# Block sums in 32-column tiles, row sums placed behind a GEMM 1 step, and the last output group in two column halves

## The chip, the core and the metric

The kernel runs on one core of a Trainium2 chip. The time is the device time of one execution in microseconds (us), the median over several executions. Beside it stands one execution that the hardware profiler recorded; all durations below are of that execution. The engines are called PE (matmuls), DVE (vector), ACT (scalar activation), POOL (GpSimd) and SP (Sync, which here only issues transfers).

## What is computed

Attention with a local part and a summary part feeds a two-layer network. There are 4 batches, 8 heads, 768 positions and 64 columns a head.

```python
k_sum = k.reshape(B, H, nb, block, D).max(axis=3)      # block = 32, nb = 24
v_sum = v.reshape(B, H, nb, block, D).mean(axis=3)
scores_l = scale * np.matmul(q, k.transpose(0, 1, 3, 2))
mask_l = np.abs(pos[:, None] - pos[None, :]) < window  # window = 16
scores_s = scale * np.einsum('bhsd,bhnd->bhsn', q, k_sum) + np.log(block)
a = softmax(np.concatenate([np.where(mask_l, scores_l, -1e9), scores_s], axis=-1))
attn = np.matmul(a, np.concatenate([v, v_sum], axis=2))
x = attn.transpose(0, 2, 1, 3).reshape(B * S, H * D)   # 3072 tokens x 512
h = x @ w_in                                           # 512 x 2048: GEMM 1
g = h * np.clip(h + 3.0, 0.0, 6.0) / 6.0
out = g @ w_out                                        # 2048 x 512: GEMM 2
```

A block's mean of v times 32 is its sum, so the kernel works with block sums of v and counts a block's weight 32 times in the denominator.

## The kernel before

**Tiles.** The 3072 tokens are 8 tiles of 384, two (the `half`s) for each batch b. Heads go in pairs p = 0 to 3, and pairs in groups g = 0 and 1. For a batch, `K` transposes k on PE, copies it into block-diagonal form (`kbd`) and takes block maxima (`red`, then `kst`); `Tq` transposes q; `Sl` makes local scores, the exponential on ACT and the mask on DVE; `Ss` makes the summary scores. `AV(b, p, half)` accumulates the numerator `num` and the denominator `den` in PSUM, takes 1/den on ACT as the exponential of a negated logarithm (lines 398 and 399) and writes x on DVE (line 400). `F1(t, ft)` is one of the 16 steps of GEMM 1 of tile t: four matmuls into `hp` (line 412), a Relu on ACT (line 415) and the product `g` on DVE (line 416). `F2` is GEMM 2: for each of three groups of 128 tokens, 16 accumulating matmuls of 512 columns (line 425), a copy on ACT (line 429) and a store that SP issues (line 431).

**Block sums of v.** They are needed as `vst[p]`, on 96 partitions (4 heads x 24 blocks) with the other heads' columns masked out, which `to_vst` does in two DVE operations (line 233). There are two ways to them.
- Batch 0: v is loaded in f32 by SP (`load_vf`, line 129) and summed on PE. `vsum0(p)` multiplies with an indicator `ind`; the two pairs of a group accumulate into an 8-partition result, in two PSUM tiles of 6 blocks' columns each. After the second pair, ACT and DVE copy one PSUM tile each into `vs8`, and SP issues one transfer that spreads it over 96 partitions, `vs96[g]` (line 266).
- Later batches: `load_vrows` brings rows of v in f32 (`vr`, 768 KB each, issued by POOL, line 136) and `vsum(b, g)` adds them up on DVE in six operations (lines 238 to 243), then calls `to_vst`. `vr` has two buffers, and `vs8` uses the same ones.

**Order of the work.** POOL's order is that of the program all the time, so a transfer that POOL issues stands behind everything that POOL is told earlier, waits included. Until line 479 the order of PE, ACT and DVE is also that of the program. After it, a planner orders these three engines. `plan` hangs pieces of attention at slots: slot 16n + i is the i-th step of the n-th entry of `work_list`, which is F1(0); F1(1) with F2(0); F2(1); F1(2); then F1(t) with F2(t-1) for t = 3 to 7; F2(7). The planner may draw a piece's instructions ahead of its slot. On every engine instructions then run in the order so fixed.

**Holding back transfers.** `hold_loads(src)` is a tiny POOL copy from `src`: POOL waits until `src` is there, and so do the transfers behind it. Before the change, line 434 waits for the last f32 piece of v; then come two pieces of w_in, the rest of q of batch 0, two pieces of w_in and four of w_out.

**PSUM.** `ps_h` (2 buffers: `hp`), `ps_o` (2 buffers: GEMM 2 results, and some `num`/`den` of batch 0), `ps_s` (2), `ps_n` (one `num`, one `den`). In batch 0, `alt` in `AV` selects `ps_o` in place of `ps_n`.

Of the kernel before, what the change touches and what calls it, by code (L numbers as in the profile page):

```python
# [16 lines left out]
D = 64  # L17
# [15 lines left out]
def kernel(  # L33
# [173 lines left out]

    ind = const.tile([128, 2, 2, 4], F32, tag="ind", name="ind")
    nc.vector.memset(ind[:], 0.0)
    for i in range(4):  # L210
        for par in range(2):
            nc.vector.memset(ind[32 * i:32 * i + 32, par, par, i:i + 1], 1.0)
    for p in range(NP):
# [31 lines left out]


    def vcast(p):
        for j in range(2):
            rows = slice(64 * j, 64 * j + 64)
            (nc.vector.tensor_copy if j else nc.scalar.copy)(vbd[p][rows, :, rows], vf[p][rows])  # L250

    vps, vs96 = {}, {}

    def vsum0(p):
        g, par = p // 2, p % 2
        for h in range(2):
            if par == 0:
                vps[g, h] = ps_n.tile([8, NK // 2, D], F32, tag=("num", "den")[h], name="vps")
            nc.tensor.matmul(vps[g, h][:], ind[:, par].rearrange("p a b -> p (a b)"),  # L259
                             vf[p][:, h * (NK // 2):(h + 1) * (NK // 2)], start=(par == 0), stop=(par == 1))  # L260
        if par == 1:
            a = ld.tile([8, NK, D], F32, tag="vr", name="vs8", bufs=2)
            for h in range(2):
                (nc.vector.tensor_copy if h else nc.scalar.copy)(a[:, h * (NK // 2):(h + 1) * (NK // 2)], vps[g, h][:])
            vs96[g] = work.tile([RS, D], F32, tag="vs96", name="vs96")
            nc.sync.dma_start(out=vs96[g][:], in_=a[:])

# [103 lines left out]
    def AV(b, p, half):  # L371
# [3 lines left out]
        a, asm = at[p], asum[b, p // 2, half]  # L375
        alt = b == 0 and (half == 0 and p != 2 or half == 1 and p % 2 == 1)
        pool = ps_o if alt else ps_n
# [24 lines left out]

    gt, ops = {}, {}

    def F1(t, ft, wide):

        if ft == 0:
            gt[t] = gp.tile([128, NFT, HALF], BF16, tag="g", name="g")
        pool, tag = (ps_o, "o") if wide and ft % 2 else (ps_h, "h")
        hp = pool.tile([128, HALF], F32, tag=tag, name="hp")  # L410
        for kt in range(NP):
            nc.tensor.matmul(hp[:], w_in_sb[:, kt, ft * 128:(ft + 1) * 128], xt[t][:, kt],  # L412
                             start=(kt == 0), stop=(kt == NP - 1))
        r = hw.tile([128, HALF], F32, tag="r", name="r")
        nc.scalar.activation(r[:], hp[:], AF.Relu, bias=half_c[:], scale=1.0 / 6.0)  # L415
        nc.vector.scalar_tensor_tensor(gt[t][:, ft], r[:], 1.0, hp[:], op0=ALU.min, op1=ALU.mult)  # L416

    def F2(t, i, by_ft=False):

        ft, ts = (i // 3, i % 3) if by_ft else (i % NFT, i // NFT)  # L420
        if ft == 0:
            pool, tag = (ps_h, "h") if by_ft and ts == 2 else (ps_o, "o")
            ops[t, ts] = pool.tile([128, d_model], F32, tag=tag, name="op")
        op = ops[t, ts]
        nc.tensor.matmul(op[:], gt[t][:, ft, ts * 128:(ts + 1) * 128], w_out_sb[:, ft],  # L425
                         start=(ft == 0), stop=(ft == NFT - 1))
        if ft == NFT - 1:
            o = hw.tile([128, d_model], F32, tag="ot", name="ot")
            nc.scalar.copy(o[:], op[:])  # L429
            row = t * HALF + ts * 128  # L430
            nc.sync.dma_start(out=out[row:row + 128], in_=o[:])


    hold_loads(vf[NP - 1][:, 0, 0:1])
    load_w_in(0)
    load_w_in(1)
    load_q(0, 0, 4, 1)
    for c in range(2, 4):
        load_w_in(c)
    for c in range(4):  # L440
        load_w_out(c)

# [4 lines left out]
    def v_first(p):  # L447
        vsum0(p)
        vcast(p)

    zero_rest()
# [9 lines left out]
    S_first(1)  # L461
    nc.vector.tensor_scalar_mul(osum4[:], hm4[:], float(BLK))
    to_vst(0, vs96[0][:])
    K(0, 2)
    v_first(2)
    Tq(0, 2, 0)
    Ss(0, 0, 0)
    v_first(3)
    K(0, 3)
    Tq(0, 3, 0)  # L470
    S_first(2)
    AV(0, 0, 0)
    S_first(3)
    to_vst(1, vs96[1][:])
    AV(0, 1, 0)
    Ss(0, 1, 0)
    AV(0, 2, 0)
# [15 lines left out]

    def attention(b, t_slot, t_gap, av_slot, av_gap, loads):
        for p in range(NP):
# [10 lines left out]
            if p % 2 == 1:  # L506
                at_slot(s + 2, lambda g=p // 2: Ss(b, g, 0))
                at_slot(s + 3, lambda g=p // 2: Ss(b, g, 1))
                at_slot(s, lambda g=p // 2: vsum(b, g))
                if b + 1 < B:  # L510
                    at_slot(s, lambda g=p // 2: load_vrows(b + 1, g))
            if 2 <= b + 1 < B:
                at_slot(s + 1, lambda p=p: (load_k(b + 1, p), load_q(b + 1, p)))
        for i, (p, half) in enumerate(((0, 0), (1, 0), (2, 0), (3, 0), (0, 1), (1, 1), (2, 1), (3, 1))):
            at_slot(av_slot(i), lambda p=p, half=half: AV(b, p, half))
# [5 lines left out]
    for g in range(2):  # L521
        at_slot(11.5, lambda g=g: (load_k(1, 2 * g, 2), load_q(1, 2 * g, 2)))
        at_slot(15, lambda g=g: load_v(1, g))
        at_slot(15, lambda g=g: load_vrows(1, g))
    attention(1, 28, 3, lambda i: (41, 42, 45, 46, 50, 52, 54, 56)[i], 2, None)
    for b in range(2, B):
        base = 48 + 32 * (b - 2)
        order = (14, 16, 24, 26, 18, 20, 28, 30)
        attention(b, base, 5, lambda i, base=base: base + order[i], 2, None)

# [42 lines left out]
```

## Time and profile before

| What | Value |
|---|---|
| Time, median of 6 runs (range) | 262.48 us (261.0 to 265.01) |
| The profiled execution: time, span | 262.66 us, 260.8 us |
| PE, ACT, DVE, POOL busy | 238.7, 167.9, 156.4, 65.3 us |
| Mean granted PE clock | 0.987 |
| GEMM 1 matmuls, 512 of 384 columns | four in 0.65 us where PE is full |
| GEMM 2 matmuls, 384 of 512 columns | three in 0.65 us where PE is full |
| First GEMM 1 matmuls of tile 0, last of tile 0 | 27.7 us, 50.5 us |
| GEMM 1 of tiles 1, 2, 3 | 50.6 to 80.0, 99.5 to 119.3, 120.1 to 149.0 us |
| GEMM 2 of tile 1 | 71.2 to 98.8 us |
| Last GEMM 2 matmul starts | 256.4 us |

The span runs from the first to the last instruction of the trace; the execution's time is measured around it and is 1.9 us longer. In the views, a row of instructions gives engine, line, operation, what it writes and reads, and in brackets how long the engine had been idle before it and what ended that. Matmul durations in the trace overlap, so the distance between starts says what PE really passes. A wait of an engine costs time only where something that sets the end stands behind it.

### The profile page before, as it was taken

The page shows a single profiled execution, that of the slowest core. Times are in us where ns is not written, and L with a number is a line of the kernel's source. Part 1 is how long each engine was busy: PE and PEld are TensorE (multiplying, and loading weights), DVE is VectorE, ACT ScalarE, POOL GpSimd, SP SyncE. Part 2 cuts the span into 40 slices and gives each one's busy share as a digit, 9 for nine tenths or more (in the row PEclk, how much of TensorE's full clock was granted, in tenths as well). Part 3 has the DMA queues.
Part 4 walks back from the last instruction along what each step waited for, and adds up shares of the span by engine and source line. Part 5 has one row for each costly group of instructions (what it writes and reads, how often), then busy time and mean ns, then how long its engine had stood idle before and what let it go on. Part 6 is the DMA issues. An engine that isn't in the chain of part 4 may idle for free.

```text
span 260.8 us, 5002 instructions
## 1 busy us (share of the span) xinstructions
PE 238.7 (92%) x1936; PEld 135.7 (52%) x1936; DVE 156.4 (60%) x362; ACT 167.9 (64%) x325; POOL 65.3 (25%) x97
## 2 busy tenths in 40 slices
PE   1775699999899979999799999999999999999993
PEld 1233456644455646666455555666655555555541
DVE  4779446633899576997994477658544444444400
ACT  8577369833687858998577557766856655555410
POOL 7219000755381501796820400000000000000000
PEclk9999679999999999999999999999999999999999
DMA  7989998599999941999991451101011111101122
GB/s 127 192 126 159 203 200 137 72 195 205 219 259 81 205 59 44 79 156 169 182 124 40 33 70 41 43 1 43 0 40 43 40 40 43 40 0 41 43 80 80
DMA packets 62711, 25.80 MB, mean 99 GB/s; under 512 B 51296, under 2 KB 58464, under 8 KB 62688
## 3 DMA queue, kind: packets, MB, share of 16 engines
q0 software_dynamic: 52752, 17.57, 60.8%
q1 hardware_dynamic: 9936, 7.92, 10.3%
q8 instruction: 15, 0.25, 0.4%
q14 instruction: 8, 0.07, 0.1%
HBM read 31.98 MB, written 6.29 MB: 147 GB/s over the span
## 4 chain that ended last, share of the span: by engine, by line
PE 66%; DMA 13%; DVE 11%; ACT 5%; issue 2%; POOL 2%; DVEq 0%; ACTq 0%; POOLq 0%
PE hp L412 26%; PE op L425 24%; DMA vr<-in_v_dram 7%; DMA vs<-vs 4%; DVE g L416 3%; PE num L382 3%; DMA qb<-in_q_dram 2%; PE num L380 2%; PE den L386 2%; PE den L389 2%; ACT r L415 2%; PE sl L344 2%; PE vps L259 1%; PE ss L354 1%; POOL vbd L120 1%
## 5 line engine op out<-in xcount | busy, mean ns | idle before, releaser
L412 PE MATMUL hp<-x,win 128*128 128x384 bf16 x512 | 105.3, 329 | 2.4 <-DVE g L416 2.0
L415 ACT ACTIVATE r<-hp,half_c 128x384 f32<-128x384 f32 x128 | 73.5, 580 | 46.4 <-PE hp L412 45.6
L425 PE MATMUL op<-wout,g 128*128 128x512 bf16 x384 | 101.0, 379 | 0.0
L416 DVE SCALAR_TENSOR_TENSOR g<-r,hp 128x384 bf16<-128x384 f32 x128 | 69.7, 551 | 46.9 <-ACT r L415 46.8
L412 PEld LDWEIGHTS <-win 128*128 128x128 bf16 x512 | 47.8, 98 | 37.1 <-issue 6.3
L425 PEld LDWEIGHTS <-g 128*128 128x128 bf16 x384 | 36.6, 98 | 32.5 <-issue 0.6
L400 DVE TENSOR_TENSOR x<-num,lg 128x384 bf16<-128x384 f32 x32 | 17.7, 554 | 23.5 <-ACT lg L399 22.2
L398 ACT ACTIVATE lg<-den 128x384 f32<-128x384 f32 x32 | 15.7, 491 | 18.4 <-PE den L393 9.9
L120 POOL DMA_DIRECT2D vbd<-in_v_dram x24 | 18.2, 779 | 36.0 <-PE num L382 32.8
L347 ACT ACTIVATE at<-sl 128x376 bf16<-128x376 f32 (+2 forms) x48 | 22.3, 487 | 5.6 <-PE sl L344 5.6
L429 ACT COPY ot<-op 128x512 f32<-128x512 f32 x24 | 13.8, 584 | 8.9 <-PE op L425 8.8
L348 DVE TENSOR_TENSOR at<-at,mask 128x376 bf16<-128x376 bf16 (+2 forms) x48 | 16.1, 348 | 3.8 <-ACT at L347 3.7
L344 PE MATMUL sl<-qT,kbd 128*128 128x94 bf16 x192 | 14.4, 207 | 3.2 <-DVE kbd L305 3.1
L399 ACT ACTIVATE lg<-lg 128x384 f32<-128x384 f32 x32 | 16.8, 525 | 0.9
L344 PEld LDWEIGHTS <-kbd 128*128 128x128 bf16 x192 | 11.7, 98 | 10.4 <-DVE kbd L305 3.4
L382 PEld LDWEIGHTS <-vbd 128*128 128x128 bf16 x224 | 13.2, 101 | 6.6 <-issue 3.2
L113 POOL DMA_DIRECT2D qb<-in_q_dram x16 | 13.4, 855 | 6.3 <-DMA vr<-in_v_dram 6.3
L382 PE MATMUL num<-at,vbd 128*128 128x94 bf16 (+2 forms) x224 | 14.4, 204 | 0.0
L113 POOL DMA_DIRECT2D kb<-in_k_dram x16 | 13.4, 852 | 0.2
L380 PE MATMUL num<-asum,vst 96*128 96x384 bf16 x32 | 10.8, 338 | 2.8 <-DVE x L400 1.6
L386 PE MATMUL den<-asum,osum 96*128 96x384 bf16 x32 | 10.7, 334 | 1.4 <-DVE x L400 1.4
L389 PE MATMUL den<-at,obd 128*128 128x384 bf16 x32 | 11.1, 345 | 0.0
(82 smaller groups left out, 206.8 us busy)
## 6 DMA issues: line engine op xcount, KB each, us to landing
out_dram<-ot SPq DMA_DIRECT2D x24, 256.0 KB, 2.0
vr<-in_v_dram POOLq DMA_DIRECT2D x6, 768.0 KB, 8.0
vbd<-in_v_dram POOLq DMA_DIRECT2D x24, 96.0 KB, 3.3
win<-in_moe_w_in_dram POOLq DMA_DIRECT2D x4, 512.0 KB, 8.9
wout<-in_moe_w_out_dram POOLq DMA_DIRECT2D x4, 512.0 KB, 17.4
vf<-in_v_dram SPq DMA_DIRECT2D x8, 192.0 KB, 8.9
kb<-in_k_dram POOLq DMA_DIRECT2D x16, 96.0 KB, 6.8
qb<-in_q_dram POOLq DMA_DIRECT2D x16, 96.0 KB, 6.4
```

Of the source, the lines that this page charges most:

```text
L113: nc.gpsimd.dma_start(out=t[:, :, j], in_=src[b, 2 * p + j].rearrange("(s p) d -> p s d", p=128))
L120: nc.gpsimd.dma_start(out=vall[rows, p, lo:hi, rows], in_=v[b, 2 * p + j].rearrange("(n k) d -> k n d", k=KB)[:, lo:hi])
L344: nc.tensor.matmul(sp[:, i * WIN:(i + 1) * WIN], kbd[p][:, t], qT[p][:, PAD - HALO + t * KB:PAD - HALO + t * KB + WIN], start=True, stop=True)
L347: nc.scalar.activation(a, sp[:, 0:n * WIN].rearrange("p (n c) -> p n c", c=WIN), AF.Exp, scale=scl)
L382: nc.tensor.matmul(num[:, lo:hi], vbd[p][:, t], a[:, t, off:off + hi - lo], start=False, stop=(i == len(bl) - 1))
L389: nc.tensor.matmul(d3, ones, a[:, t0:t1, HALO:HALO + KB], start=False, stop=False)
L399: nc.scalar.activation(lg[:], lg[:], AF.Exp, scale=-1.0)
L400: nc.vector.tensor_tensor(xt[s][:, p], num[:], lg[:], op=ALU.mult)
L412: nc.tensor.matmul(hp[:], w_in_sb[:, kt, ft * 128:(ft + 1) * 128], xt[t][:, kt], start=(kt == 0), stop=(kt == NP - 1))
L415: nc.scalar.activation(r[:], hp[:], AF.Relu, bias=half_c[:], scale=1.0 / 6.0)
L416: nc.vector.scalar_tensor_tensor(gt[t][:, ft], r[:], 1.0, hp[:], op0=ALU.min, op1=ALU.mult)
L425: nc.tensor.matmul(op[:], gt[t][:, ft, ts * 128:(ts + 1) * 128], w_out_sb[:, ft], start=(ft == 0), stop=(ft == NFT - 1))
```

## The change

- `ind` becomes 128 x 32, with one column in eight used. For each pair and each half of a head's 64 columns, `vsum0` makes one matmul into its own 32 partitions of one PSUM tile per group (tag `num` for group 0, `den` for group 1); nothing accumulates over pairs. One ACT copy of 128 x 384 takes the result, and two transfers of 32 columns each bring every eighth partition to `vs96[g]`. POOL issues them, except the first of group 1, which SP issues.
- The weight loads and the rest of q wait for both halves of `vs96[1]` in place of the last f32 piece of v.
- In the hand-ordered start, `to_vst(0)` moves behind K(0, 2), both `v_first(2)` and `v_first(3)` behind Ss(0, 0, 0), AV(0, 0, 0) and AV(0, 1, 0) forward, and `to_vst(1)` behind Ss(0, 1, 0). `alt` is true where p % 2 equals half, so consecutive pairs use different PSUM pools.
- `vsum` has slots of its own and may no longer be drawn ahead of the DVE operation of the GEMM 1 step that was told last (`issue_after`). Batch 1: 36 and 39 for 35 and 41; batch 2: 52.5 and 56.5 for 57 and 67; batch 3: 68.5 and 78.5 for 89 and 99. Both `load_vrows` of a batch stand at one slot: 12 for 15 (batch 1), 45 for 35 and 41 (batch 2), 60 for 57 and 67 (batch 3).
- The last token group of GEMM 2 is 32 matmuls of 256 columns, one column half after the other, each with its own PSUM tile, copy and store. The last half is copied by ACT and DVE together.

```diff
-    ind = const.tile([128, 2, 2, 4], F32, tag="ind", name="ind")
+    ind = const.tile([128, 32], F32, tag="ind", name="ind")
     nc.vector.memset(ind[:], 0.0)
     for i in range(4):
-        for par in range(2):
-            nc.vector.memset(ind[32 * i:32 * i + 32, par, par, i:i + 1], 1.0)
+        nc.vector.memset(ind[32 * i:32 * i + 32, 8 * i:8 * i + 1], 1.0)
...
     def vsum0(p):
         g, par = p // 2, p % 2
+        if par == 0:
+            vps[g] = ps_n.tile([128, NK, D // 2], F32, tag=("num", "den")[g], name="vps")
         for h in range(2):
-            if par == 0:
-                vps[g, h] = ps_n.tile([8, NK // 2, D], F32, tag=("num", "den")[h], name="vps")
-            nc.tensor.matmul(vps[g, h][:], ind[:, par].rearrange("p a b -> p (a b)"),
-                             vf[p][:, h * (NK // 2):(h + 1) * (NK // 2)], start=(par == 0), stop=(par == 1))
+            c = 2 * h + par
+            nc.tensor.matmul(vps[g][32 * c:32 * c + 32], ind[:], vf[p][:, :, h * (D // 2):(h + 1) * (D // 2)],
+                             start=True, stop=True)
         if par == 1:
-            a = ld.tile([8, NK, D], F32, tag="vr", name="vs8", bufs=2)
+            a = ld.tile([128, NK, D // 2], F32, tag="vr", name="vs8", bufs=2)
+            nc.scalar.copy(a[:], vps[g][:])
+            vs96[g] = work.tile([RS, D], F32, tag="vs96", name="vs96")
             for h in range(2):
-                (nc.vector.tensor_copy if h else nc.scalar.copy)(a[:, h * (NK // 2):(h + 1) * (NK // 2)], vps[g, h][:])
-            vs96[g] = work.tile([RS, D], F32, tag="vs96", name="vs96")
-            nc.sync.dma_start(out=vs96[g][:], in_=a[:])
+                (nc.sync if g == 1 and h == 0 else nc.gpsimd).dma_start(
+                    out=vs96[g][:, h * (D // 2):(h + 1) * (D // 2)], in_=a[64 * h:64 * h + 64:8])
...
-        alt = b == 0 and (half == 0 and p != 2 or half == 1 and p % 2 == 1)
+        alt = b == 0 and p % 2 == half
...
-        nc.vector.scalar_tensor_tensor(gt[t][:, ft], r[:], 1.0, hp[:], op0=ALU.min, op1=ALU.mult)
+        last_g[0] = nc.vector.scalar_tensor_tensor(gt[t][:, ft], r[:], 1.0, hp[:], op0=ALU.min, op1=ALU.mult)
...
+        if t == NTILE - 1 and ts == HALF // 128 - 1:
+            F2_last(op, row, ft)
+            return
...
-    hold_loads(vf[NP - 1][:, 0, 0:1])
-    load_w_in(0)
-    load_w_in(1)
-    load_q(0, 0, 4, 1)
-    for c in range(2, 4):
-        load_w_in(c)
-    for c in range(4):
-        load_w_out(c)
+    def F2_last(op, row, step):
+
+        t, w, ts_last = NTILE - 1, d_model // 2, "last"
+        for n in (2 * step, 2 * step + 1):
+            h, ft = n // NFT, n % NFT
+            cols = slice(h * w, (h + 1) * w)
+            if n == NFT:
+                ops[t, ts_last] = ps_h.tile([128, w], F32, tag="h", name="op")
+            p = op[:, 0:w] if h == 0 else ops[t, ts_last][:]
+            nc.tensor.matmul(p, gt[t][:, ft, HALF - 128:], w_out_sb[:, ft, cols],
+                             start=(ft == 0), stop=(ft == NFT - 1))
+            if ft == NFT - 1:
+                o = hw.tile([128, d_model], F32, tag="ot", name="ot")
+                if h == 0:
+                    nc.scalar.copy(o[:, 0:w], p)
+                else:
+                    nc.scalar.copy(o[:, 0:w // 2], p[:, 0:w // 2])
+                    nc.vector.tensor_copy(o[:, w // 2:w], p[:, w // 2:])
+                nc.sync.dma_start(out=out[row:row + 128, cols], in_=o[:, 0:w])
...
     def v_first(p):
         vsum0(p)
         vcast(p)
+        if p == NP - 1:
+            hold_loads(vs96[1][:, 0:1])
+            hold_loads(vs96[1][:, D // 2:D // 2 + 1])
+            load_weights()
...
+    K(0, 2)
     to_vst(0, vs96[0][:])
-    K(0, 2)
-    v_first(2)
     Tq(0, 2, 0)
     Ss(0, 0, 0)
+    v_first(2)
     v_first(3)
+    AV(0, 0, 0)
     K(0, 3)
     Tq(0, 3, 0)
     S_first(2)
-    AV(0, 0, 0)
+    AV(0, 1, 0)
     S_first(3)
+    Ss(0, 1, 0)
     to_vst(1, vs96[1][:])
-    AV(0, 1, 0)
-    Ss(0, 1, 0)
     AV(0, 2, 0)
     AV(0, 3, 0)
...
+    def vsum_in_turn(b, g):
+        with tc.issue_after(last_g[0].ins):
+            vsum(b, g)
...
-                at_slot(s, lambda g=p // 2: vsum(b, g))
-                if b + 1 < B:
-                    at_slot(s, lambda g=p // 2: load_vrows(b + 1, g))
...
+        for g in range(2):
+            at_slot(sums[g], lambda g=g: vsum_in_turn(b, g))
+            if b + 1 < B:
+                at_slot(rows, lambda g=g: load_vrows(b + 1, g))
...
-        at_slot(15, lambda g=g: load_vrows(1, g))
-    attention(1, 28, 3, lambda i: (41, 42, 45, 46, 50, 52, 54, 56)[i], 2, None)
+        at_slot(12, lambda g=g: load_vrows(1, g))
+    attention(1, 28, 3, lambda i: (41, 42, 45, 46, 50, 52, 54, 56)[i], (36, 39), 45)
...
-        attention(b, base, 5, lambda i, base=base: base + order[i], 2, None)
+        attention(b, base, 5, lambda i, base=base: base + order[i], (base + 4.5, base + 8.5) if b == 2 else (base - 11.5, base - 1.5), base + 12)
```

`load_weights()` issues the same loads in the same order as the removed lines.

More of the change, by code (lines that the diff above doesn't have):

```diff
@@ L403 @@
     gt, ops = {}, {}
+    last_g = [None]
     def F1(t, ft, wide):
@@ L424, in F2 @@
         op = ops[t, ts]
+        row = t * HALF + ts * 128
+        if t == NTILE - 1 and ts == HALF // 128 - 1:
+            F2_last(op, row, ft)
+            return
         nc.tensor.matmul(op[:], gt[t][:, ft, ts * 128:(ts + 1) * 128], w_out_sb[:, ft],
@@ L429, in F2, with load_weights @@
             nc.scalar.copy(o[:], op[:])
-            row = t * HALF + ts * 128
             nc.sync.dma_start(out=out[row:row + 128], in_=o[:])
-    hold_loads(vf[NP - 1][:, 0, 0:1])
-    load_w_in(0)
-    load_w_in(1)
-    load_q(0, 0, 4, 1)
-    for c in range(2, 4):
-        load_w_in(c)
-    for c in range(4):
-        load_w_out(c)
+    def F2_last(op, row, step):
[16 more added lines that the diff above has]
+                nc.sync.dma_start(out=out[row:row + 128, cols], in_=o[:, 0:w])
+    def load_weights():
+        for c in range(2):
+            load_w_in(c)
+        load_q(0, 0, 4, 1)
+        for c in range(2, 4):
+            load_w_in(c)
+        for c in range(4):
+            load_w_out(c)
     def S_first(p):
@@ L492, with attention @@
         at_slot(12 + p, lambda p=p: AV(0, p, 1))
-    def attention(b, t_slot, t_gap, av_slot, av_gap, loads):
+    def vsum_in_turn(b, g):
+        with tc.issue_after(last_g[0].ins):
+            vsum(b, g)
+    def attention(b, t_slot, t_gap, av_slot, sums, rows):
         for p in range(NP):
```

## Prediction, made before the changed kernel ran

> **What bounds the kernel now.** I read four views, in this order: the busy table by stages, the chain that ended last, the list of waits, and the timeline around the waits. The busy table by stage says which engine is short where (columns: stage in us and its length; busy us and, in brackets, instructions of PE, weight loads, DVE, ACT, POOL; granted clock; DMA share; GB/s).
>
> ```profile
> 20.00:32.40 12.40, 7.53 (x99) 5.26 (x99) 8.31 (x20) 6.85 (x14) 5.47 (x8) 0.85 1.15 187
> 32.40:50.00 17.60, 17.42 (x186) 10.66 (x185) 10.81 (x22) 14.26 (x30) 2.58 (x5) 0.91 0.82 131
> 68.00:85.00 17.00, 16.77 (x163) 9.08 (x163) 15.91 (x38) 13.99 (x27) 7.74 (x10) 1.00 1.63 175
> 85.00:100.00 15.00, 13.26 (x140) 7.92 (x136) 9.07 (x24) 11.08 (x23) 3.53 (x5) 1.00 0.80 110
> 100.00:120.00 20.00, 19.76 (x204) 13.51 (x202) 18.52 (x44) 18.10 (x39) 14.98 (x20) 1.00 1.25 119
> 120.00:143.00 23.00, 21.66 (x172) 12.94 (x170) 17.52 (x41) 15.63 (x33) 8.53 (x11) 1.00 1.32 122
> 200.00:246.00 46.00, 46.00 (x259) 24.53 (x258) 19.77 (x36) 24.68 (x45) 0.00 (x0) 1.00 0.09 35
> ```
>
> From 143 us on PE is full: nothing but fewer PE instructions helps there, and the change has none. PE has holes at the start (7.53 of 12.40 us before GEMM 1 runs) and in 85 to 100 and 120 to 143. The second thing to see is DVE in 100 to 120: 18.52 of 20 us, no room. The chain that ended last and the waits name what makes the holes.
>
> ```profile
> 13.88 4.96 DMA vs<-vs
> 22.84 6.07 DMA vs<-vs
> ```
>
> (start and length in us; both stand in the chain) and
>
> ```profile
> DVE vr L238 <- DMA vr<-in_v_dram: 5.1, 3, 2.3
> DVE vst L233 <- DMA vs<-vs: 3.0, 2, 1.6
> PE num L380 <- DVE x L400: 1.6, 1, 1.6
> PE den L386 <- DVE x L400: 1.4, 1, 1.4
> ```
>
> (total us, times, longest). Two kinds of DMA (the batch-0 block sums `vs`, the row loads `vr`) stand in front of DVE, which works in order, and PE waits for what DVE has queued behind. In the timeline:
>
> ```profile
> 28.93 0.49 DVE L233 TENSOR_TENSOR vst<-vs,hm 96x128 bf16<-96x128 f32 x2 [1.58 <-DMA vs<-vs]
> 91.08 0.69 DVE L238 TENSOR_TENSOR vr<-vr 96x512 f32<-96x512 f32 x1 [2.29 <-DMA vr<-in_v_dram]
> 94.29 0.32 PE L380 MATMUL num<-asum,vst 96*128 96x384 bf16 x1 [1.63 <-DVE x L400]
> 125.38 0.81 PE L412 MATMUL hp<-x,win 128*128 128x384 bf16 x4 [1.34 <-DVE g L416]
> 256.89 0.59 ACT L429 COPY ot<-op 128x512 f32<-128x512 f32 x1 [2.91 <-PE op L425]
> 257.50 0.33 SPq L431 DMA_DIRECT2D out_dram<-ot  x1
> ```
>
> **Part 1, the start, up to x of tile 0 (34.3 us now: L400 starts at 33.75 and takes 0.56).** I follow DVE, which carries this stretch. Up to 17.5 us (end of `osum4`) nothing changes. Now: 1.38 us of waiting for `vs96[0]`, `to_vst(0)`, K(0,2), casts, the 0.55 us copy L264, K(0,3), masks, x, 1.58 us for `vs96[1]`, `to_vst(1)`, then x of pairs 1, 2, 3, with waits of 2.27 and 1.03 us for ACT. After:
> - K(0,2) needs 0.96 + 0.96 + 0.28 = 2.2 us, to 19.7; `to_vst(0)` 0.49, to 20.2; two casts of 0.56, to 21.3. The wait of 1.38 us is gone if `vs96[0]` lands by 19.7. It is copied by 13.75 (ACT has the copy, 0.47 us, behind its masks' exponentials); POOL is idle then (9.46 us of idle end at 18.30) and issues two DMAs at about 0.75 us each, to 15.3. Landing: 2.0 us by the output stores' row, so 17.3.
> - The first x comes before K(0,3) now and pays for its own logarithm and exponential: AV 20.5 to 21.3, ACT copies and casts until 21.8, 0.49 + 0.53, so x at 22.8 to 23.35. That is a new idle of 1.5 us on DVE.
> - K(0,3) to 25.6, masks to 26.2, x of pair 1, 26.7, masks, 27.3, `to_vst(1)`, 27.8 without waiting; AV of pair 2 takes 0.8, ACT 1.0, x to 30.2; pair 3 to 31.3. The wait of 1.35 us of `den` for x (25.41 to 26.93) goes, since pairs alternate between the two PSUM pools.
> So 31.3 for 34.3: 3.0 us less. The granted clock was half from 28.6 to 35.4 us in this trace; if that comes again at the same place, the last two AVs take twice as long and 2.3 is left. I take **2.7**.
>
> What the part adds: the weight loads stand behind `vs96[1]` now. The block sums' matmuls end at about 20.5 (four records of one `v_first` took 1.46 us from 18.66), copy to 21.0, DMA to 23.3, two POOL copies of 0.18: the first load is issued at 23.5, for 18.77 now, **4.7 us later**. Queued behind that wait on POOL are all eight weight loads and the rest of q, and they fill the DMA engines for 23 us (20.6 to 43.9, at about 205 KB of landed data a us). First w_in piece: 18.8 + 5.5 + 4.7 = 29.0, before x at 31.3. Rest of q (issued 20.26, 8.8 to landing): 33.8; its transposes start 2.25 us behind the last x now, so at 33.6: level. Last w_in piece: 34.1 + 4.7 = 38.8, needed some 9 us into GEMM 1, at 40. Covered, with a us to spare at most; bounds 0 and +3 us (Tq at 33.8 + 3 = as now).
>
> **The rule against it**: the Trainium skill, "DMA: Bandwidth & Descriptors", "Issuing engine by pattern", gives simple copies to Sync, and its table of latencies about 1 us to the first byte for GpSimd's queue and 0.6 for Sync's. By that rule, moving three of four pieces costs 0.4 us each. By the row above the same 24 KB took 4.96 us on SP, because its queue still carried the f32 loads of v until 17.9 us (the DMA view shows 256-byte packets until then), and 6.07 beside the weights. I go by the row: the price of the queue is what stood in it.
>
> A second one: "TensorEngine Tiling (Array Packing)", "Key Properties", says that a change of tiling mode drains TensorE; 32-column tiles would pay it eight times. The nearest row is 64-column transposes followed by full-width matmuls: sixteen of 96 columns start at 82.08 and GEMM 2 at 82.55. Sixteen in turn would be 0.64 us at 40 ns, pairs side by side 0.32; so tiles do overlap, and at most 0.15 us is left for a switch. Eight are 1.2 us at most, against 4 x 0.73 saved where two tiles overlap too (bounds: 0 and 2.9 us of PE). PE waits for DVE here, so I book zero; the `ind` memsets and the DVE copy of 0.55 are in the sums above.
>
> **Part 2, the row sums (vr).** One `vsum` is 3 x 0.68 + 0.42 + 0.28 + 0.22 = 2.96 us of DVE and 0.56 for `to_vst`. Now they are drawn ahead by the planner, to 64.3, 72.2, 79.7, 91.1, 122.6 and 130.8 us, where DVE waits for three of the loads. From the distance of each matmul's start to the next I subtracted its streaming time (0.42 ns a column, as four 384-column matmuls pass in 0.65 us): PE loses 0.86 us at 65.1, 1.80 at 92.3 and 1.50 at 123.7. These go, as the loads come earlier (batch 1: slot 12 for 15, ahead of the v loads; batches 2 and 3: both at one slot, behind sums that are done) and the sums come later: 4.2 us.
> What is late next: both sums of batch 1 move behind the last GEMM 1 step of tile 1 (80 us), into a stretch with 15 us and 9.07 of DVE, 3 us of which leave: room. Both sums of batch 2 move to slots 52.5 and 56.5, that is into 104 to 112 us, where DVE has 1.5 us free and gets 5.9 more. 24.4 us of DVE do not fit in 20. Some 4 us must be drawn ahead or pushed back; PE can go on with GEMM 2 steps meanwhile, but g comes later and GEMM 1 has two PSUM buffers. Cover for one late 0.68 us operation is the other buffer (0.65 us of matmuls). Bounds: 0, and 5.9 - 1.5 = 4.4. At 68 to 85 DVE was 94% busy and PE lost about 1 us in all, so I take **1.5**. The sums of batch 3 move to 127 and 147, where DVE has room. Sum: 4.2 - 1.5 = **2.7** less.
>
> **Part 3, the tail.** The same 16 x 512 columns as 32 x 256: by streaming time 107 ns each where it is 216 now; a weight load is 98 ns, beside them. The first half's copy and store lie under 1.7 us of matmuls. The last copy: ACT and DVE 128 columns each, about 0.28 us by the line through ACT's 282 and 470 columns (404 and 562 ns) and DVE's 96x128 row, for 0.59. The store's packets ran from 258.34 to 259.17; half the bytes take 0.4 less, or nothing, if issue decides: 0.2. **0.5** less.
>
> **Sum.** 2.7 + 2.7 + 0.5 = 5.9. The profiled execution took 262.66 us (span 260.8), the median of six is 262.48; from the profiled one, 262.66 - 5.9 = **256.8 us**, and the span about 254.9.
>
> **Rivals.**
> 1. The DVE-heavy stage gives back all of part 2 (4.4 us of cost for 4.2): 262.66 - 2.7 - 0.5 + 0.2 = 259.7. For it: 18.52 of 20 us busy. Against it: PE has other work. 17%.
> 2. The weights are the new wait: q and w_in hold PE at the start, and part 1 gives nothing: 262.66 - 3.2 = 259.5. For it: margins of about a us. Against it: GEMM 1 takes 1.1 us a step with attention between, slower than pieces land. 13%.
> 3. **Slower**: a sum stays in one piece behind its GEMM 1 step, 3.5 us ahead of the next g. Two PSUM buffers cover 1.2, so each of the four sums of batches 2 and 3 costs 2.3: 9.2 in all, and 262.66 - 5.9 + 9.2 - 1.5 = 264.5. It decides from 1.9 us a sum on (7.4 us of gains over four). For it: the order is now forced. Against it: the planner may still put g between the nine operations, as it does at 130 to 134 us. 8%.
> 4. Nothing moves: too many independent parts for that, 3%.
>
> My forecast has 59%, with 253.5 to 258.8 of its own. The range is 252.5 (start unthrottled, no cost on DVE, 1 us more) to 261.0 (1 and 2 half together with a cost more). Within 0.5% (1.3 us), about what this kernel's measurement can tell, is 261.2 to 263.8. Faster 0.88, same 0.05, slower 0.07.
>
> **What would show it.** Right: no DVE wait for `vs`, both transfers about 2.5 us, the last x of tile 0 near 31 us; no wait of L238's successor for `vr`; DVE nearly full in 100 to 120 with PE slack under 3.5 us; the last ACT copy near 0.3 us. Wrong: transposes of q waiting for their DMA past 35 us; PE idle before GEMM 1 matmuls for g behind row sums; block-sum transfers that still take 5 us.

## The result, and the profile after

| | before | after |
|---|---|---|
| Median (range) | 262.19 us (259.76 to 266.8, 72 runs) | 261.26 us (259.02 to 262.45, 35 runs) |
| Profiled execution: time, span | 262.66, 260.8 us | 260.9, 259.0 us |
| GEMM 1 of tile 0 (start of its first and of its last matmul, as in the next four rows) | 27.7 to 50.5 | 28.1 to 49.4 |
| GEMM 1 of tile 1 | 50.6 to 80.0 | 49.5 to 77.8 |
| GEMM 2 of tile 1 | 71.2 to 98.8 | 68.0 to 95.2 |
| GEMM 1 of tile 2 | 99.5 to 119.3 (19.8 us) | 95.9 to 119.1 (**23.2 us**) |
| GEMM 1 of tile 3 | 120.1 to 149.0 | 119.8 to 147.3 |
| Start of the last GEMM 1 matmul of tile 7 to the end of the span | 15.3 | 15.1 |

The ratio of the times is 0.9972 [0.9957, 0.9987]: about 0.7 us less, within the half per cent that the prediction counts as no change. Ratios, here and below, leave out executions more than 1.5% above the fastest of their kernel, and medians do not, so a ratio need not be the quotient of two medians (of the 22 executions of `double`, below, it leaves out 9). The forecast was 256.8 us, and its range ended at 261.0.

The table shows where time was gained and lost. The changed kernel gains 1.1 us by the end of GEMM 1 of tile 0, 2.2 by the end of tile 1 and 3.6 by the start of tile 2. Then 20 us later the gain is 0.2. It comes back to 1.7 at tile 3, and the span ends 1.8 us earlier. (One execution differs from the next by about a us, so the last digit of these is not the median's.)

The waits that were to go are gone. Of the four lines of the list of waits that the prediction quotes, none is left as it was; these stand in the list of the kernel after (total us, times, longest):

```profile
PE hp L414 <- DVE g L418: 1.5, 2, 1.3
PEld L414 <- DMA win<-in_moe_w_in_dram: 1.3, 1, 1.3
PE hp L414 <- DMA win<-in_moe_w_in_dram: 0.6, 1, 0.6
```

No DVE operation waits for `vr` or `vs` any more. The waits for w_in are new. PE waited for `g` before, too (2.0 us in all, longest 1.3), but the long one has moved, from 125.4 us into the stage of GEMM 1 of tile 2. Both are met again below. The busy table by stage, for the stages that changed (columns as in the prediction):

```profile
20.00:32.00 12.00, 10.40 (x101) 6.92 (x100) 5.77 (x14) 6.38 (x14) 7.72 (x12) 1.00 0.76 124
81.00:96.00 15.00, 14.94 (x153) 8.87 (x151) 11.28 (x31) 12.39 (x27) 1.40 (x2) 1.00 0.50 137
96.00:119.50 23.50, 20.81 (x200) 13.62 (x197) 22.09 (x52) 18.60 (x39) 15.84 (x21) 1.00 1.13 90
119.50:141.00 21.50, 21.50 (x180) 13.08 (x177) 16.51 (x38) 15.44 (x32) 7.75 (x10) 1.00 1.22 143
```

The holes of PE in the stages before and behind GEMM 1 of tile 2 are closed: 14.94 of 15 us and 21.50 of 21.50. Between them PE now has 20.81 of 23.5, and DVE has 22.09. PE's holes have moved into the stage where DVE is full. In 20 to 32 PE looks busier than before with about as many instructions (101 for 99 in 20 to 32.4): that is no more work, but slower matmuls, as the section on the clock shows.

The timeline at the start, in order of time (start and length in us; what had kept the engine idle, in brackets):

```profile
22.67 1.60 POOL L144 DMA_DIRECT2D win<-in_moe_w_in_dram  x2
27.23 0.48 DVE L232 TENSOR_TENSOR vst<-vs,hm 96x128 bf16<-96x128 f32 x2
27.51 0.49 ACT L358 ACTIVATE asum<-ss 96x384 bf16<-96x384 f32 x1 [0.59 <-PE ss L355]
28.11 1.46 PE L414 MATMUL hp<-x,win 128*128 128x384 bf16 x4 [0.64 <-DMA win<-in_moe_w_in_dram]
29.36 0.53 PE L381 MATMUL num<-asum,vst 96*128 96x384 bf16 x1
30.89 0.27 PE L394 MATMUL den<-at,obd 128*128 128x75 bf16 x1
32.27 0.56 DVE L401 TENSOR_TENSOR x<-num,lg 128x384 bf16<-128x384 f32 x1 [4.56 <-ACT lg L400]
33.27 0.56 DVE L401 TENSOR_TENSOR x<-num,lg 128x384 bf16<-128x384 f32 x1 [0.44 <-ACT lg L400]
```

`to_vst(1)` (L232) starts at 27.23 without waiting, as predicted (27.3). AV of pair 2 (L381 to L394) could follow on PE at 28.0, when ACT has written `asum`. But four matmuls of GEMM 1 of tile 0 stand ahead of it in PE's order. They wait 0.64 us for the first piece of w_in, which is issued at 22.67 now and at 18.77 before, and then take 1.25 us to pass. So AV starts at 29.36 and ends at 31.16. DVE is idle 4.56 us, and the last x is done at 33.8, for the 31.3 of the prediction and 34.3 before.

The timeline in the full stage, around the longest waits of PE in it (DVE's rows, then PE's):

```profile
106.69 0.56 DVE L308 COPY kbd<-tp 64x768 bf16<-64x768 bf16 x1
107.28 0.29 DVE L242 TENSOR_TENSOR vr<-vr 96x128 f32<-96x128 f32 x1
107.60 0.96 DVE L312 TENSOR_REDUCE red<-tp 128x24 bf16<-128x768 bf16 x1
108.47 0.21 DVE L242 TENSOR_TENSOR vr<-vr 96x64 f32<-96x64 f32 x1
108.61 0.17 DVE L321 TENSOR_TENSOR kst<-red,hmk 128x48 bf16<-128x48 bf16 x1
108.70 0.54 DVE L418 SCALAR_TENSOR_TENSOR g<-r,hp 128x384 bf16<-128x384 f32 x1
...
109.30 0.81 PE L414 MATMUL hp<-x,win 128*128 128x384 bf16 x4 [1.26 <-DVE g L418]
118.19 0.48 PE L355 MATMUL ss<-qT,kst 128*96 128x384 bf16 x2 [1.10 <-DVE red L312]
```

DVE goes from one operation to the next without idling, additions of the row sum (L242) between those of K, and this `g` starts 3.8 us after the one before it (104.91 us). PE has no free `hp` buffer and waits 1.26 us. Behind the second row sum of the batch PE waits 1.10 us more, for a `red`.

### The profile page after: what moved, and what is told of

Read it like the earlier page. It is cut to its first block, busy times and chain, and to the rows that moved or that the text cites. A ratio compares the mean times of both kernels' runs of the same rounds, so it can differ in the third digit from the quotient of the medians.

```text
span 259.0 us, 5035 instructions
## 1 busy us (share of the span) xinstructions
PE 240.4 (93%) x1952; PEld 139.4 (54%) x1952; DVE 155.1 (60%) x357; ACT 168.0 (65%) x326; POOL 67.5 (26%) x101
## 4 chain that ended last, share of the span: by engine, by line
PE 74%; DVE 11%; DMA 6%; ACT 5%; issue 2%; SPq 1%; POOL 0%; ACTq 0%; POOLq 0%
PE op L431 29%; PE hp L414 27%; DMA vf<-in_v_dram 3%; PE sl L345 3%; PE num L383 3%; DVE g L418 3%; DMA win<-in_moe_w_in_dram 2%; PE ss L355 2%; PE num L381 2%; PE den L387 2%; PE den L390 2%; DVE red L312 1%; ACT r L417 1%; PE vps L259 1%; PE tp L336 1%
## 5 line engine op out<-in xcount | busy, mean ns | idle before, releaser
L431 PE MATMUL op<-wout,g 128*128 128x512 bf16 x368 | 98.3, 379 | 0.0
L431 PEld LDWEIGHTS <-g 128*128 128x128 bf16 x368 | 35.2, 98 | 30.4 <-issue 0.6
L345 PEld LDWEIGHTS <-kbd 128*128 128x128 bf16 x192 | 12.5, 103 | 9.1 <-DVE kbd L306 1.8
L400 ACT ACTIVATE lg<-lg 128x384 f32<-128x384 f32 x32 | 16.8, 526 | 0.9
L435 ACT COPY ot<-op 128x512 f32<-128x512 f32 x23 | 13.2, 586 | 5.9 <-PE op L431 5.7
L345 PE MATMUL sl<-qT,kbd 128*128 128x94 bf16 x192 | 15.4, 216 | 1.6 <-DVE kbd L306 1.6
L381 PE MATMUL num<-asum,vst 96*128 96x384 bf16 x32 | 11.2, 350 | 0.5 <-DVE vst L232 0.4
L297 PE MATMUL tp<-ident,kb 96*64 96x96 bf16 x128 | 5.8, 245 | 5.5 <-DMA kb<-in_k_dram 5.5
## 6 DMA issues: line engine op xcount, KB each, us to landing
out_dram<-ot SPq DMA_DIRECT2D x23, 256.0 KB, 2.0
```

Source lines behind the costliest of these rows:

```text
L345: nc.tensor.matmul(sp[:, i * WIN:(i + 1) * WIN], kbd[p][:, t], qT[p][:, PAD - HALO + t * KB:PAD - HALO + t * KB + WIN], start=True, stop=True)
L381: nc.tensor.matmul(num[:], vst[p][:].rearrange("p h d -> p (h d)"), asm[:], start=True, stop=False)
L400: nc.scalar.activation(lg[:], lg[:], AF.Exp, scale=-1.0)
```

## The experiments

Theory A on the start: x of tile 0 is held by GEMM 1 matmuls that were drawn ahead and wait for w_in. Theory B on the row sums: the predicted 4.2 us are gained, and nearly as much is paid in the stage of GEMM 1 of tile 2, because DVE has no room there. Theory C on the clock comes with the third group.

### Each part of the change by itself

Three kernels have one part of the change each: the whole start with the block sums (`p1_start`), the slots, loads and `issue_after` of the row sums (`p2_sums`), and the last token group (`p3_tail`). The core of the second, against the kernel before:

```diff
-                at_slot(s, lambda g=p // 2: vsum(b, g))
-                if b + 1 < B:
-                    at_slot(s, lambda g=p // 2: load_vrows(b + 1, g))
...
+        for g in range(2):
+            at_slot(sums[g], lambda g=g: vsum_in_turn(b, g))
+            if b + 1 < B:
+                at_slot(rows, lambda g=g: load_vrows(b + 1, g))
```

> The kernel before with only the start of the change: 32-column block sums, the new order, the alternating PSUM pools and the weight loads behind the block sums. Theory A (weights and PE order hold the start: in the changed kernel's profile four GEMM 1 matmuls stand before AV of pair 2 and wait for w_in): the last x of tile 0 ends 0.3 to 1 us earlier than in the kernel before, last GEMM 1 step of tile 0 about 1 us earlier, time 0 to 1 us lower. Rival (the start gives the 2.7 us of the prediction and the middle eats it): time 2 to 3 us lower.

> The kernel before with only the new places of the row sums and row loads. Theory B (what is gained between 64 and 99 us and at 124 us is given back in the stage of GEMM 1 of tile 2, where DVE is full): that stage is 3 to 3.5 us longer than the 19.8 us of the kernel before, the stages ahead of it 2.5 us shorter, the one behind it 1.3 us shorter; time 0 to 1 us lower. Rival (the start spoils it): time 2.5 us lower or more.

> The kernel before with only the two column halves at the end. All theories: last copy 0.29 us for 0.59, last store's packets about 0.3 us shorter; time 0.2 to 0.5 us lower.

Against the kernel before, measured beside them:

| | median, us | ratio |
|---|---|---|
| `p1_start` | 261.33 | 0.9983 [0.9956, 1.0011] |
| `p2_sums` | 261.79 | 1.0008 [0.9988, 1.0027] |
| `p3_tail` | 261.07 | 0.9992 [0.9964, 1.002] |

None can be told from no change. The start alone shows the same picture as the whole change (timeline of `p1_start`):

```profile
28.15 1.46 PE L414 MATMUL hp<-x,win 128*128 128x384 bf16 x4 [0.42 <-DMA win<-in_moe_w_in_dram]
29.41 0.53 PE L381 MATMUL num<-asum,vst 96*128 96x384 bf16 x1
```

Its last x is done at 34.0 and GEMM 1 of tile 0 at 49.5, one us sooner than before. The row sums alone lengthen GEMM 1 of tile 2 to 23.3 us (96.6 to 119.9; 19.8 before) and have DVE busy for 21.73 of them: what they save ahead of it and behind it, they pay there. So the full stage is not a product of the new start.

### The full stage without its row sums, and with them spread out

`no_sums2` leaves out the six additions of each of the two row sums of batch 2; `to_vst` then works on rows that were not added up, and the block sums of batch 2 are missing from the output.

```diff
     def vsum(b, g):
         r, w = vr_t[b, g], BLK // PCS * D
+        if b == 2:
+            to_vst(g, r[:, 0, 0:D])
+            return
```

> The changed kernel with the six additions of both row sums of batch 2 left out (only the masking stays, on unsummed rows), so 5.9 us of DVE are gone from the stage of GEMM 1 of tile 2. Theory B: that stage falls from 23.2 to 20 us, the time by 3 to 3.5 us. Rival (PE order or POOL sets this stage's length): under 1 us.

Measured: 258.59 us, 0.9882 [0.9842, 0.9921], and 19.7 us for GEMM 1 of tile 2. Without these additions (5.9 us of DVE) the stage is as short as it was before the change, and the kernel is about 0.9% faster than the one after: 2.4 us, for the 3 to 3.5 expected.

`balance` leaves nothing out. The additions of batch 2 go to slots 41 and 44, their `to_vst` stays at 52.5 and 56.5, and so that the rows are there, batch 1's sums go to 26 and 33 and the loads for batch 2 to 34.

```diff
-            at_slot(sums[g], lambda g=g: vsum_in_turn(b, g))
+            if b == 2:
+                at_slot((41, 44)[g], lambda g=g: vsum_in_turn(b, g, 0))
+                at_slot(sums[g], lambda g=g: vsum_in_turn(b, g, 1))
+            else:
+                at_slot(sums[g], lambda g=g: vsum_in_turn(b, g))
...
-    attention(1, 28, 3, lambda i: (41, 42, 45, 46, 50, 52, 54, 56)[i], (36, 39), 45)
+    attention(1, 28, 3, lambda i: (41, 42, 45, 46, 50, 52, 54, 56)[i], (26, 33), 34)
```

> The changed kernel with the row sums of batch 1 at slots 26 and 33 for 36 and 39, the row loads of batch 2 at 34 for 45, and the additions of batch 2 at slots 41 and 44, ahead of the stage of GEMM 1 of tile 2 (only the masking stays at 52.5 and 56.5). Nothing is left out. Theory B: that stage falls from 23.2 to about 20 us, the stages ahead grow by at most 1 us, and the time is 2 to 3 us lower than the changed kernel's. Rival (what leaves one stage overfills another): under 1 us.

Measured: 259.41 us, 0.9878 [0.9844, 0.9912], about 2.4 us less than the kernel after; the stage takes 20.8 us. The busy table of the exact stage, first to last GEMM 1 matmul of tile 2, in five kernels, one row each. The kernel before:

```profile
99.50:119.30 19.80, 19.56 (x202) 13.27 (x198) 18.12 (x42) 17.90 (x39) 14.28 (x19) 1.00 1.16 115
```

The kernel after:

```profile
95.90:119.10 23.20, 20.51 (x196) 13.44 (x194) 21.70 (x52) 18.30 (x39) 15.44 (x20) 1.00 1.13 88
```

`p2_sums`:

```profile
96.60:119.90 23.30, 20.59 (x198) 13.45 (x194) 21.73 (x52) 18.34 (x40) 15.58 (x20) 1.00 1.16 97
```

`no_sums2`:

```profile
96.20:115.90 19.70, 19.46 (x199) 13.38 (x197) 18.32 (x43) 17.77 (x39) 14.35 (x19) 1.00 1.30 98
```

`balance`:

```profile
96.70:117.50 20.80, 19.99 (x205) 13.67 (x204) 18.77 (x45) 18.18 (x39) 16.55 (x22) 1.00 1.69 119
```

ACT's busy time hardly moves and PE's by about one us; DVE's moves most, and the length goes with it: DVE is busy 92, 94, 93, 93 and 90% of the stage. **With 3.6 us more of DVE's work the stage is 3.4 us longer, and with this work taken out or placed elsewhere it is short again, or nearly.** In the short stages of the kernel before and of `no_sums2` PE is busy 99% of the time, and the lists of waits show none of PE there. In the kernel after and in `p2_sums` PE waits 1.3 us for `g` and 1.1 us for `red`, both of DVE. So DVE sets the length of the long stages, while in the short ones PE is full as well. Theory B holds, as far as this stage goes.

`no_turn` asks for the opposite: it keeps the slots and drops the tie to the last `g`, so the planner may draw the sums ahead again.

```diff
     def vsum_in_turn(b, g):
-        with tc.issue_after(last_g[0].ins):
-            vsum(b, g)
+        vsum(b, g)
```

> The changed kernel without the rule that keeps the row sums behind a GEMM 1 step; the slots stay, and the planner draws the additions ahead again. Theory B: the stage of GEMM 1 of tile 2 falls to about 20 us again; as the rows are loaded earlier than in the kernel before, DVE waits for them less, so the time is 1 to 3 us lower than the changed kernel's. Rival (the waits for row loads return): DVE waits of 1 to 2 us for vr as before, and no gain over the changed kernel.

Measured: 266.28 us, 1.0149 [1.0086, 1.0212], slower than the kernel before. The stage is back at 19.7 us, as theory B has it, but the time is not, since the waits for rows return. List of waits of `no_turn`:

```profile
DVE vr L237 <- DMA vr<-in_v_dram: 5.7, 3, 4.2
PE hp L414 <- DVE g L418: 4.8, 2, 4.2
```

One row sum of batch 1 is drawn ahead to where its rows are 4.2 us from landing, and `g`, and with it PE, stands behind it. The time fits the rival of the expectation. So the tie is needed with these slots; what costs is the place that batch 2's sums were given.

### The start: what stands ahead on PE, and when w_in is issued

`order` keeps the first four GEMM 1 steps of tile 0 behind the last AV of that tile. `early_w` puts the weights back behind the last f32 piece of v, as in the kernel before, and has SP issue both transfers of group 1, so that they don't stand behind the weights on POOL. Their cores, in this order:

```diff
+    def F1_behind(t, ft, wide):
+        with tc.issue_after(last_av[0].ins):
+            F1(t, ft, wide)
...
-                F1(f1, i, f2 is None)
+                (F1_behind if f1 == 0 and i < 4 else F1)(f1, i, f2 is None)
```
```diff
-                (nc.sync if g == 1 and h == 0 else nc.gpsimd).dma_start(
+                (nc.sync if g == 1 else nc.gpsimd).dma_start(
...
-        vsum0(p)
-        vcast(p)
         if p == NP - 1:
-            hold_loads(vs96[1][:, 0:1])
-            hold_loads(vs96[1][:, D // 2:D // 2 + 1])
+            hold_loads(vf[NP - 1][:, 0, 0:1])
             load_weights()
+        vsum0(p)
+        vcast(p)
```

> The changed kernel with the first four GEMM 1 steps of tile 0 kept behind AV of pair 3 on PE. Theory A (four GEMM 1 matmuls stand ahead of AV of pair 2, wait for w_in and delay it by 1.5 us): AV of pair 2 starts at 27.8 us for 29.4, the last x of tile 0 ends about 1.2 us earlier, at 32.6 for 33.8, time 0.5 to 1.2 us lower than the changed kernel's. Rival (x is held by ACT and DVE, or the last w_in piece decides): no change.

> The changed kernel with the weight loads released as in the kernel before, by the last f32 piece of v, and both transfers of group 1's block sums on SP, beside the weights. Theory A, part 2 (w_in lands too late for the GEMM 1 matmuls that stand ahead): these no longer wait, AV of pair 2 starts about 0.6 us earlier, time 0.3 to 1 us lower. Rival (the block sums then take 6 us beside the weights, as in the kernel before): DVE waits for them until 27 us or later, and the time is the same or higher than the changed kernel's.

| | median, us | ratio | weights issued | last x done | last GEMM 1 matmul of tile 0 starts |
|---|---|---|---|---|---|
| after | 261.26 | 0.9972 [0.9957, 0.9987] | 22.67 | 33.8 | 49.4 |
| `order` | 259.75 | 0.9902 [0.9878, 0.9927] | 23.46 | 32.3 | 48.8 |
| `early_w` | 259.18 | 0.9898 [0.9868, 0.9928] | 18.25 | 31.8 | 47.4 |

Both ways of freeing AV bring about 0.7% against the kernel after, and neither interval touches its. In `order` the next wait shows at once (timeline of `order`):

```profile
28.69 0.32 PE L382 MATMUL num<-asum,vst 96*128 96x384 bf16 x1 [0.57 <-DVE vst L232]
34.94 0.43 PE L336 MATMUL tp<-ident,qb 36*64 36x36 bf16 x16 [1.45 <-DMA qb<-in_q_dram]
```

AV of pair 2 is released by `vst` now, not by w_in, although in that execution everything had begun 1 us later; then q, which is queued with the weights, is late. In `early_w` that wait is not there, but the transfers of group 1 share the DMA engines with the weights, take about 8 us, and DVE waits for them (timeline of `early_w`):

```profile
27.86 0.49 DVE L232 TENSOR_TENSOR vst<-vs,hm 96x128 bf16<-96x128 f32 x2 [0.71 <-DMA vs<-vs]
28.21 0.34 PE L381 MATMUL num<-asum,vst 96*128 96x384 bf16 x1 [0.89 <-DVE vst L232]
```

0.71 us of waiting here is cheaper than weights 4.4 us later. Theory A holds in that the matmuls drawn ahead hold AV back in the kernel after. What that alone is worth is not shown: both kernels also come to the full clock sooner in their traces (26.7 and 25.6 us, for 31.3), which is the subject of the next group, and these runs do not separate the two.

### The clock at the start

The page gives no change of the granted clock in the kernel after, but the matmuls do. This is the same denominator matmul (384 columns) of two pairs, in the timeline of the kernel after:

```profile
24.49 0.53 PE L390 MATMUL den<-at,obd 128*128 128x384 bf16 x1
31.74 0.34 PE L390 MATMUL den<-at,obd 128*128 128x384 bf16 x1
```

And in the timeline of the kernel before:

```profile
22.64 0.34 PE L389 MATMUL den<-at,obd 128*128 128x384 bf16 x1
30.37 0.53 PE L389 MATMUL den<-at,obd 128*128 128x384 bf16 x1
```

After runs at half speed from the first matmul until 31.3 us (the first clock record of its trace, and before it the page prints 1.00 for want of one). Before was granted full speed at 11.6 and fell to half from 28.6 to 35.4. Theory C: the tiles of 32 columns pass side by side, so PE has less to do at the start, and it is this that holds the clock down. `double` issues every block-sum matmul twice, with the same result.

```diff
-            nc.tensor.matmul(vps[g][32 * c:32 * c + 32], ind[:], vf[p][:, :, h * (D // 2):(h + 1) * (D // 2)],
-                             start=True, stop=True)
+            for _ in range(2):
+                nc.tensor.matmul(vps[g][32 * c:32 * c + 32], ind[:], vf[p][:, :, h * (D // 2):(h + 1) * (D // 2)],
+                                 start=True, stop=True)
```

> The changed kernel with every matmul of the block sums issued twice in a row (the second overwrites the first with the same values), so that PE does as much for them as in the kernel before. In the three profiles with 32-column block sums the granted clock stayed at half from the start to 31.3 to 31.6 us; in the three with the old block sums it rose at 11.6 to 13.0 us. Theory C (the overlapping 32-column tiles take so little of PE that the clock is not raised): the clock rises by 13 us; matmuls at the start pass in half the time, and the time falls by up to 1 us. Rival (it is something else at the start, such as the order): the clock still rises after 30 us, and the time is the same or up to 0.7 us higher.

The clock rose at 10.4 us, as theory C has it, but the time did not fall: 264.17 us, 1.0039 [1.0012, 1.0066]. The weights were issued 0.7 us later still, PE came sooner to the GEMM 1 matmuls and waited longer for them, and during this wait the clock went down again (27.4 to 34.3 us). Timeline of `double`:

```profile
29.98 1.46 PE L415 MATMUL hp<-x,win 128*128 128x384 bf16 x4 [4.01 <-DMA win<-in_moe_w_in_dram]
31.24 0.52 PE L382 MATMUL num<-asum,vst 96*128 96x384 bf16 x1
```

Neither expectation on the time fits. The quicker PE found the same late w_in.

The mean granted clock of every execution is on record, too. In the kept traces whose clock rose late it is 0.998 or more, because the slow start has no record; in the others it is 0.967 to 0.993. Counted by this sign, which is inferred for executions without a kept trace, 49 of 92 executions of the kernels with the 32-column matmuls issued once rose late, none of the 38 executions with every one issued twice, and 5 of 127 with the old block sums. So theory C holds for the clock, as a tendency. No gain in time shows: in the kernel after, the 23 executions that rose late have a median of 261.38 us, and the 13 others, which lost clock later, 261.23. The start of `no_turn` has the same instructions as that of the kernel after. Its clock rose at 12.0 us, PE waited 3.85 us for w_in, and its last x was done at 34.8 us. In it and in `double` the clock was down again by then, and AV of pair 2 ran at half speed as in the kernel after.

### Putting the remedies together

`both` is `early_w` with `balance`. `both_order` adds `order`, and `both_double` adds `order` and `double`; their edits are those shown.

> The changed kernel with the early weight loads of early_w and the moved row sums of balance; nothing is left out. If the two give-backs are separate (the start: about 0.7% of the time, the stage of GEMM 1 of tile 2: about 0.9%), they add: ratio to the kernel before about 0.980 to 0.982. If they are one wait seen twice, no better than 0.988.

> As both, and GEMM 1 of tile 0 stays behind AV of pair 3 on PE as in order. Theory A: with w_in in time, the GEMM 1 matmuls that stand ahead cost nothing, so no more than 0.3 us either way against both. Rival (PE order costs by itself): about 1 us lower than both.

> As both_order, with every block-sum matmul issued twice. In double the granted clock rose at 10.4 us, and PE then waited 4.0 us for w_in. With that wait gone the higher clock should show alone. Theory C is worth something: 0.3 to 1 us lower than both_order. Rival (DVE sets the start, so PE's clock there is free): within 0.3 us, or higher by the 1.5 us that the doubled matmuls of pairs 2 and 3 take ahead of the copy.

| | median, us | ratio |
|---|---|---|
| `both` | 257.05 (256.0 to 258.55) | 0.982 [0.9767, 0.9874] |
| `both_order` | 258.62 | 0.9868 [0.9813, 0.9923] |
| `both_double` | 259.46 | 0.9912 [0.9882, 0.9942] |

`both` is **faster than the kernel before and the one after**, and by what its two halves bring alone: 0.9898 x 0.9878 / 0.9972 = 0.980. The last GEMM 1 matmul of tile 0 starts at 47.7 us in it, and GEMM 1 of tile 2 takes 21.4, with DVE busy for 19.3. With the weights there in time, holding GEMM 1 back (`both_order`) no longer helps, and by the medians costs 1.6 us, although the intervals overlap; neither expectation fits. In its trace GEMM 1 starts only at 31.7, and PE, with less to do until then, is at half speed until 35.0. `both_double` has the full clock at 12.2 us, loses it again from 29.3 to 32.7, and gains nothing on `both_order`, as its rival had it.

## Why the prediction was wrong

**The start, 2.7 us: the failed step is the sum along DVE.** "I follow DVE, which carries this stretch", and "First w_in piece: 29.0, before x at 31.3 ... Covered". DVE's own part came as written: no wait for `vs`, `to_vst(1)` at 27.23 for 27.3, the first x at 22.7 for 22.8. (The transfers of group 0 took 5.1 and 5.4 us, for 2.0 written, while loads of v still passed on SP's queue until 16.8 us and loads of k and q on POOL's until 14.1. That is a sign named for being wrong, but nothing waited for them.) The first piece of w_in even came sooner than written: its matmuls start at 28.1. But w_in was priced against the x that GEMM 1 needs, and not against what stands behind the GEMM 1 matmuls on PE. PE works in order, and the planner had drawn these matmuls ahead of AV of pair 2. The timeline of the kernel before showed it:

```profile
27.67 0.49 PE L412 MATMUL hp<-x,win 128*128 128x384 bf16 x2
29.28 0.50 PE L380 MATMUL num<-asum,vst 96*128 96x384 bf16 x1 [1.11 <-DVE vst L233]
```

There w_in was early, AV waited for `vst`, and the order cost nothing.

The last x came 2.5 us later than written (33.8 for 31.3). The trace splits this in two. AV of pair 2 starts 1.6 us late (29.4 for 27.8), mostly because of the wait for w_in (0.64 us) and the 1.25 us in which the four matmuls pass. And this AV takes 1.8 us (29.36 to 31.16) for the 0.8 written, because PE is at half speed. The four matmuls would pass in 0.65 us at full speed, so half speed is about 1.6 of the 2.5 us (an estimate from these rows). The prediction foresaw it for the two last AVs ("2.3 is left"), and booked 0.3 us for it; that the earlier matmuls would be at half speed too was not foreseen.

Of the 2.7 us, 1.1 came in the profiled execution. By the median of the part alone it is about 0.4 (0.17% of 261.75), which cannot be told from nothing. `order` and `early_w` get more out of the start, with AV freed and the clock up sooner; their shares stay open.

**The row sums, 2.7 us: the failed term is "I take 1.5".** The gain was right: 4.2 predicted; in the stages, 1.1 over tile 1, 1.4 up to the start of tile 2 and 1.5 between the ends of tiles 2 and 3, 4.0 in all. The cost was 3.4 for 1.5, with a bound of 4.4. The sum to take was written in the text ("24.4 us of DVE do not fit in 20"); the discount rested on a stage at 94% DVE that lost about 1 us, and that stage had as much DVE work as fitted. All twelve additions ran in the full stage (103.7 to 115.9 us). 2.3 us of other DVE work left it (5.9 came and DVE rose by 3.6), and the 3.6 cost nearly their full length, as the five rows above show. The reason given for the discount was "PE can go on with GEMM 2 steps meanwhile". In this stage there are none: GEMM 2 of tile 1 ends at 95.2 us and that of tile 2 starts at 121.1 (the entry F1(2) of the work list has no F2 beside it), so PE waits for `g` and `red`.

**The tail, 0.5 us: 0.3 came, and not from the copy.** About 0.3 us were to come from the copy and 0.2 from the store. The 32 half-width matmuls pass in 3.66 us, and each half of the last copy takes less than 0.3, as written. But DVE's half starts 0.30 us behind ACT's, so the two do not overlap: 0.59 us from 255.40 to 255.99, which is what the one copy took before (the same 0.59 in `p3_tail`). What runs them in turn is open. The 0.3 us that came are the store's: its packets pass in 0.53 us (256.85 to 257.38), for 0.83 before. Timeline of the kernel after:

```profile
251.67 3.66 PE L447 MATMUL op<-wout,g 128*128 128x256 bf16 x32
255.40 0.27 ACT L454 COPY ot<-op 128x128 f32<-128x128 f32 x1 [1.38 <-PE op L447]
255.70 0.29 DVE L455 COPY ot<-op 128x128 f32<-128x128 f32 x1 [10.22 <-DMA out_dram<-ot]
```

**The rivals.** Rival 1 (the full stage gives part 2 back) happened for the most part, with a cost of 3.4 of 4.4 us. Of rival 2 (w_in is the new wait) the size came, 1.6 of 2.7 us lost at the start, and the wait in part: the rest is half speed. Together and in full they give 259.5 + 2.9 = 262.4; the profiled execution took 260.9. They were weighed as alternatives, 17% and 13%, and lie in different stages, so that both can come: their joint case is what the upper end of the range had to reach, and the range, which counted half of each and "a cost more", ended at 261.0. Rival 3 (a sum in one piece ahead of `g`) did not come: the planner put other operations between the additions, and the longest wait for a `g` was 1.3 us.

By its own terms: 2.7 became 1.1, 2.7 became 4.0 - 3.4 = 0.6, 0.5 became 0.3. Sum 2.0, for 1.8 in the two spans.

## What to carry to other kernels

When a transfer is put off, look at the first instruction that waits for it and at everything queued behind that instruction on its in-order engine, not only at the consumer for whose sake the data is loaded. When work is moved out of a wait into another stage, add up the busy table of that stage after the move: where one engine is then the fullest and the others have no other work, the stage grows by nearly the whole of what that engine gets more (3.4 us for 3.6 here, at 94% busy). When a kernel's matmuls are priced, ask at which clock they will run; the rows of the kernel before hold for its clock alone. Two mishaps in different stages are a case of their own; a range has to hold their sum.

## What was not expected of the hardware

**Less work on PE at the start tends to keep its clock down.** Nine kernels have the 32-column block sums issued once. In the traces of eight, matmuls run at half speed from the beginning until 25.5 to 35.0 us; the ninth (`no_turn`) rose at 12.0. All five with the old block sums, or with `double`'s, rose between 10.4 and 13.0 us. Over all executions it is about half against hardly any, as counted above. The tiles do pass side by side: eight records of them took 1.64 us at half speed, where four of the same number of columns took 2.73 us at half speed before, which makes 3.3 times the pace. Timelines of the kernel after and of the kernel before:

```profile
17.73 1.64 PE L259 MATMUL vps<-vf,ind 128*32 128x384 f32 x8
8.56 2.73 PE L259 MATMUL vps<-vf,ind 128*8 128x384 f32 x4
```

What an earlier full clock would be worth with the weights there in time stays open: where it was raised on purpose, more matmuls were the price, and where w_in was late, the clock fell again while PE waited for it (`double`, `no_turn`).
